# Unread matmuls in seven places of a convolution and mixture-of-experts kernel's head, and a longer SP turn in its planner's account

## The chip, the cores and the metric

The kernel runs on one core of one Trainium2 chip. The metric is device time in microseconds (us) from one execution's start to its end, the median over runs. PE is TensorE (the matrix engine), DVE VectorE, ACT ScalarE, POOL GpSimd and SP SyncE, whose queue issues most of the transfers here.

## The reference

Two steps follow each other. First a causal depthwise convolution of seven taps over 8 sequences of 3584 tokens with 192 channels, whose taps are a softmax of a small weight per head. Then a mixture of experts: each of the 28,672 convolved tokens goes to the one expert of eight with the highest cosine logit, and is weighted by its softmax probability.

```python
x_unf = x_pad[:, idx, :].reshape(B, S, K, H, group)
out = np.einsum('hk,bskhg->bshg', w, x_unf)
...
logits = xn @ en.T / tau
expert_idx = np.argmax(logits, axis=1)
gate_w = probs[np.arange(N), expert_idx]
for e in range(E):
    mask = expert_idx == e
    h = np.maximum(x[mask] @ w1[e], 0.0)
    out[mask] = gate_w[mask, None] * (h @ w2[e])
```

Here `w1` is 192 x 1024 and `w2` 1024 x 192 for each expert.

## The kernel before

The tokens are cut into 16 chunks of 1792. A chunk is convolved on PE against band matrices (`conv`), squared and scaled (`square`, `scales`, `scaled`), split into a high and a low half-precision part (`rest`), transposed, and multiplied by the expert embeddings (`logits`, line 772). `rank` makes ranks and destinations of the logits, and POOL scatters the rows into the DRAM table `rows_d`, sorted by expert. Expert blocks read them back transposed (`rows_of`, line 931) into `xr` or `work`, multiply them by `w1` (line 1100, `h_ps`) and `w2` (line 1122, `o_ps`), and POOL scatters the results to the output (line 1130).

**The head.** The first chunks, the preparation of eight experts' weights and the first eight expert blocks stand in an order written out by hand, the string `HEAD`. Each of its words is one small step: `1c6` is a convolution of chunk 1, `ax1` to `ax3` the trace of a weight's squares and its exponents (expert `a`, lines 369 to 384), `bh1` and `bl1` the high and low parts of a weight, `1t20` a PE transpose, `0g3` a group of logits, `1k3` a stage of the ranks, `z2p0` half of an expert block's first layer, `W6` a weight load. Within each engine the instructions keep the order of the string.

**After the head.** `run` hands out expert blocks step by step and keeps a clock of its own, `self.clock`, that counts PE's planned time. Between the steps it draws pieces of the chunks' routes from `dispatch`. In `route` a chunk's rows are transposed by transfers on SP's queue (`turn`, line 782), and the logits of a group wait, in the plan, until the clock has reached the group's due time:

```python
due[g] = self.queue(SP_TURN, SP_WAIT) + SP_LAND
...
yield due[0]
```

`queue` adds `SP_TURN` to a running time at which SP is free. The plan fixes the order of PE's stream only; on the chip PE waits for the landing itself when the logits come too soon. The account has no other use than these due times, and the due times of chunk 2, whose transposes stand at the end of the head, are zero.

Fourteen matmuls of 128 x 128 by 256 columns that nobody reads stand before the head already (`warm`, line 1262). PSUM is split into rings: `h` with six banks, `l` with one, and `r` with one, which in the kernel before is first used by the convolutions drawn from `dispatch`.

Of the kernel before, what the change touches and what calls it, by code (L numbers as in the profile page):

```python
# [12 lines left out]
F16 = mybir.dt.float16  # L13
F32 = mybir.dt.float32
# [42 lines left out]
SOON = 13  # L57
RANK, GAP = 10.0, 0.5
PE_CONV, PE_LG = 0.64, 0.3
SP_FETCH, SP_TURN, SP_X, SP_WAIT, SP_LAND = 2.8, 2.9, 1.5, 2.5, 3.4  # L60
RAW = 2 * (2 * F + F * D // 128)
AREAS = (1, 2), (1, 1), (1, 0), (0, 1), (1, 1), (1, 0), (0, 1)
HEAD = ("0c0 0c2 0c1 0c5 0c7 0c4 0c6 0c3 0q3 0q7 0q4 0q1 ax1 0q5 0q2 ax2 0q0 0q6 0p "
# [12 lines left out]
AHEAD = 0.4  # L76
HALF = 3 * 2048
SETTLE = 6.0
# [11 lines left out]
def _dep(tc, frm, to, sync=True):  # L90
    cls = mybir.DependencyClass.Sync if sync else mybir.DependencyClass.NoSync
    tc.add_manual_dep(
        frm, to, mybir.DependencyInfo(cls, mybir.DependencyReason.DATA),
        reason="routed rows are written before they are read",
    )
# [15 lines left out]
class _Moe:  # L111
# [473 lines left out]
    def head(self, v):  # L585
        k, a = v[0], v[1:]
        if k in "012":
            c, k, a = int(k), v[1], v[2:]
            if k == "c":
                self.conv(c, int(a), "h")  # L590
            elif k == "q":
                for t in (2 * int(a), 2 * int(a) + 1):
                    self.square(c, t, c or int(a) % 2 == 0)
            elif k == "p":
                self.scales(c)
            elif k == "s":
                self.scaled(c, int(a))
            elif k == "r":
                self.rest(c, int(a))
            elif k == "t":  # L600
                self.flip(c, int(a[0]), int(a[1]))
            elif k == "g":
                if c not in self.lgs:
                    self.lgs[c] = self.ps("l", [128, NT, 2 * E], F32, "lg_ps")
                self.logits(self.lgs[c], self.tiles[c, int(a)], int(a))
            elif k == "v":
                self.roots[c] = self.root(self.mixed[c][3][:])
            elif k == "f":
                self.mixed[c] += self.factor(c),
            else:  # L610
                if k == "k" and a == "1":
                    self.ranks[c] = self.rank(c, self.lgs[c], self.mixed[c][4])
                next(self.ranks[c], None)
        elif k in "abcdefgh":
            e, n = "abcdefgh".index(k), int(a[1])
            if a[0] != "x":
                (self.high if a[0] == "h" else self.low)(e, n - 1)
            elif n < 3:
                self.trace(e, n - 1)
            else:  # L620
                self.exponents(e)
        elif k == "X":
            self.load_x(int(a))
        elif k == "T":
            self.turned = [self.turn(2, g) for g in range(NT // GX)]
        elif k == "W":
            n = int(a)
            self.prep_load(min(n, 7), n - 7 if n > 6 else None)
        elif k == "F":
            self.first_rows("AB".index(a))  # L630
        else:
            e = int(a[0])
            if e not in self.zs:
                self.zs[e] = self.first_block(e)
            next(self.zs[e])


    def rank(self, c, lg, f):
        nc, sp = self.nc, self.sp
# [77 lines left out]
    def by_tile(self, r32):  # L717
# [4 lines left out]
        for i, w in enumerate((self.oneh, self.lth)):  # L722
            nc.tensor.matmul(out=fl(pc[:, 1 - i]), lhsT=w[:TP, :], rhs=fl(self.ohh),
                             start=True, stop=True)
        nc.vector.tensor_copy(out=tot[:, :, 0], in_=self.cb)
        nc.scalar.copy(out=tot[:, :, 1:], in_=pc[:, 1])
        nc.vector.tensor_tensor_scan(out=fl(run), data0=fl(rst), data1=fl(tot),
                                     initial=0.0, op0=ALU.mult, op1=ALU.add)
        have, n = run[:, :, SOON], float(PHASES[1])
# [512 lines left out]
    def run(self):  # L1242
# [15 lines left out]
            self.prep_load(e)  # L1258
        self.embeddings(em, tb)
        warm = self.ps("h", [128, 256], F32, "warm")  # L1260
        for _ in range(WARM):
            i = self.nc.tensor.matmul(out=warm, lhsT=self.idh, rhs=self.onef.bitcast(F16),
                                      start=True, stop=True)
            _dep(self.tc, i.ins, self.em_last, False)
        at = len(self.nc.cur_bb.bb.instructions)
# [11 lines left out]
        a = self.dispatch()  # L1277
# [4 lines left out]
        live, due, done, out = next(a, None), [0.0, 0.0], False, 0.0  # L1282
        while live or self.pend or not done or self.at < len(self.subs):
            if self.at < len(self.subs):
# [5 lines left out]
                for v in self.expert():  # L1290
                    self.steer(spent)
                    self.clock += self.dt
                    out = min(1.0, out + self.pace)
# [54 lines left out]
```

## Time and profile before

| | |
|---|---|
| runs before | 1244.38, 1250.32, 1250.33 us; median 1250.32 us |
| the profiled execution | 1250.26 us, its span 1248.5 us, mean granted clock 0.965 |
| PE busy | 1131.0 us, 91% of the span, in 11202 matmuls |
| DVE, ACT, POOL busy | 642.7, 605.5, 525.3 us |
| transfers | 146.58 MB; share of time of the 16 DMA engines by queue: 38.9% and 14.6% |

The granted clock is the share of TensorE's full clock (2.4 GHz) that the chip allowed: 1.00 is 2.4 GHz and 0.50 is 1.2 GHz, the only two levels here; a value between is a mean over both. Matmuls overlap, so one's duration is longer than the distance to the next; a group's time over its count gives the pace. In rows of the timeline the bracket at the end says how long the engine had been idle before and what it waited for.

### The profile page before, as it was taken

The page shows a single profiled execution, that of the slowest core. Times are in us where ns is not written, and L with a number is a line of the kernel's source. Part 1 is how long each engine was busy: PE and PEld are TensorE (multiplying, and loading weights), DVE is VectorE, ACT ScalarE, POOL GpSimd, SP SyncE. Part 2 cuts the span into 40 slices and gives each one's busy share as a digit, 9 for nine tenths or more (in the row PEclk, how much of TensorE's full clock was granted, in tenths as well). Part 3 has the DMA queues.
Part 4 walks back from the last instruction along what each step waited for, and adds up shares of the span by engine and source line. Part 5 has one row for each costly group of instructions (what it writes and reads, how often), then busy time and mean ns, then how long its engine had stood idle before and what let it go on. Part 6 is the DMA issues. An engine that isn't in the chain of part 4 may idle for free.

```text
span 1248.5 us, 28836 instructions
## 1 busy us (share of the span) xinstructions
PE 1131.0 (91%) x11202; PEld 899.9 (72%) x11202; DVE 642.7 (51%) x1734; ACT 605.5 (49%) x1480; POOL 525.3 (42%) x553
## 2 busy tenths in 40 slices
PE   5775998888989999999999998958999999999997
PEld 3575876667868777667777776736777778788886
DVE  5985656455546456474664646512433344455452
ACT  5984466446445564545554654313444443334332
POOL 3446145445554454555535553563121212222222
PEclk8887999999999999999999999968999999999999
DMA  9968447885996945967678476332022213231210
GB/s 252 277 115 207 102 87 169 168 175 104 183 187 115 192 101 131 202 123 163 133 156 189 90 141 121 85 90 66 24 52 58 52 40 65 58 66 35 51 48 24
DMA packets 324306, 146.58 MB, mean 117 GB/s; under 512 B 266126, under 2 KB 314637, under 8 KB 324160
## 3 DMA queue, kind: packets, MB, share of 16 engines
q1 hardware_dynamic: 300496, 93.97, 38.9%
q0 software_dynamic: 23664, 50.68, 14.6%
q8 instruction: 89, 1.46, 0.5%
q14 instruction: 57, 0.47, 0.1%
HBM read 38.35 MB, written 51.05 MB: 72 GB/s over the span
## 4 chain that ended last, share of the span: by engine, by line
PE 63%; issue 12%; DVE 7%; ACT 5%; DMA 4%; another core or an unknown queue 3%; POOL 3%; SPq 0%; POOLq 0%; ACTq 0%; DVEq 0%
PE h_ps L1100 29%; PE o_ps L1122 26%; PE conv_ps L445 5%; POOL out_dram L1130 3%; DMA xtb<-rows 3%; ACT work L1104 2%; DVE work L1107 2%; DVE res L406 2%; DVE xt L522 1%; PE lg_ps L772 1%; ACT sq L457 1%; DMA xr<-rows_d 1%; ACT rows L527 1%; ACT res L402 0%
## 5 line engine op out<-in xcount | busy, mean ns | idle before, releaser
L1107 DVE SCALAR_TENSOR_TENSOR work<-h_ps,work 128x384 f16<-128x384 f32 (+1 forms) x536 | 320.3, 608 | 494.6 <-ACT work L1104 388.5
L1122 PEld LDWEIGHTS <-work 128*128 128x128 f16 x5472 | 459.8, 98 | 102.2 <-issue 50.2
L1122 PE MATMUL o_ps<-res,work 128*128 128x192 f16 x4992 | 465.5, 248 | 53.3 <-issue 31.1
L1100 PEld LDWEIGHTS <-res 128*128 128x128 f16 x3520 | 310.1, 99 | 163.4 <-issue 25.7
L1104 ACT ACTIVATE work<-h_ps 128x384 f16<-128x384 f32 (+1 forms) x536 | 277.6, 533 | 275.9 <-PE h_ps L1100 200.9
L1130 POOL DMA_INDIRECT out_dram<-y,ids x200 | 203.6, 1018 | 396.2 <-ACT y L1127 366.9
L793 POOL DMA_INDIRECT rows_d<-rows,di x256 | 256.9, 1004 | 183.2 <-ACT work L1104 74.4
L1100 PE MATMUL h_ps<-xr,res 128*128 128x384 f16 (+3 forms) x2280 | 329.6, 300 | 3.2 <-issue 1.6
L1127 ACT ACTIVATE y<-o_ps,gs 128x192 f32<-128x192 f32 x200 | 83.0, 419 | 240.6 <-PE o_ps L1122 175.1
L1100 PE MATMUL h_ps<-work,res 128*128 128x384 f16 (+2 forms) x1240 | 167.7, 288 | 5.8 <-issue 5.7
L445 PE MATMUL conv_ps<-xt,band 128*112 128x384 f32 x256 | 108.3, 514 | 1.3 <-ACT xt L448 0.6
L448 ACT COPY xt<-conv_ps 112x384 f32<-112x384 f32 x128 | 60.7, 480 | 74.8 <-PE conv_ps L445 40.8
L457 ACT ACTIVATE sq<-xt 112x192 bf16<-112x192 f32 x196 | 70.8, 361 | 3.7
L1130 POOL DMA_INDIRECT out_dram<-y,e_mt x20 | 28.1, 1406 | 82.3 <-ACT y L1127 79.5
L522 DVE TENSOR_TENSOR xt<-xt,x_p_s 112x768 f32<-112x768 f32 x64 | 58.7, 946 | 0.0
L527 ACT CAST rows<-xt 112x768 f16<-112x768 f32 x64 | 52.7, 828 | 11.8 <-DVE xt L522 7.2
L534 DVE TENSOR_TENSOR rows<-xt,rows 112x512 f16<-112x512 f32 x64 | 43.9, 686 | 14.2 <-ACT rows L527 9.9
L445 PEld LDWEIGHTS conv_ps<-xt,band 128*112 128x112 f32 x256 | 39.2, 184 | 10.0 <-issue 3.7
L772 PEld LDWEIGHTS <-xtb 128*128 128x128 f16 x768 | 27.7, 96 | 23.6 <-DMA xtb<-rows 13.5
L772 PE MATMUL lg_ps<-ma,xtb 128*128 128x16 f16 x512 | 28.2, 170 | 12.0 <-DMA xtb<-rows 9.4
L457 ACT ACTIVATION_READ_ACCUMULATOR sq<-xt 112x1 f32 x196 | 37.3, 190 | 0.0
L460 DVE SCALAR_TENSOR_TENSOR sq<-xt 112x192 bf16<-112x192 f32 x60 | 21.4, 357 | 19.1 <-ACT xt L448 17.7
(201 smaller groups left out, 651.3 us busy)
## 6 DMA issues: line engine op xcount, KB each, us to landing
xt<-in_dram SPq DMA_DIRECT2D x8, 1536.0 KB
xt<-in_dram SPq DMA_DIRECT2D x7, 1440.0 KB
res<-in_dram SPq DMA_DIRECT2D x6, 768.0 KB
rows_d<-rows,di POOLq DMA_INDIRECT x256
out_dram<-y,ids POOLq DMA_INDIRECT x200
res<-in_dram SPq DMA_DIRECT2D x5, 512.0 KB
xr<-rows_d SPq DMA_TRANSPOSE x154
work<-in_dram SPq DMA_DIRECT2D x3, 512.0 KB
```

The lines of the kernel that those rows point to most:

```text
L445: self.behind(nc.tensor.matmul(out=ps, lhsT=self.band[h], rhs=xt[:, :, h * G:(h + 1) * G], start=True, stop=True))
L457: nc.scalar.activation(out=sq, in_=xc[:, t, :], func=AF.Square, accum_out=n2[:, t:t + 1])
L522: self.nc.vector.tensor_tensor(out=xc[:, u, :], in0=xc[:, u, :], in1=sb, op=ALU.mult)
L527: self.nc.scalar.copy(out=rows[:, u, 128:128 + D], in_=xc[:, u, :])
L772: i = self.nc.tensor.matmul(out=lg[:, g * GX + a, :], lhsT=xT[:, u:u + 128], rhs=self.mb if k == 2 else self.ma, start=(k == 0), stop=(k = ...
L793: i = self.nc.gpsimd.indirect_dma_start(out=self.rows_d[:, :], out_offset=bass.IndirectOffsetOnAxis(ap=idx, axis=0), in_=src, in_offset=No ...
L1100: mm = nc.tensor.matmul(out=ps[:, c, :], lhsT=wa[:, o:o + 128], rhs=xT[:, k, :], start=(i == 0), stop=(i == 4))
L1104: self.step = nc.scalar.activation(out=hh[:, b:b + m, :], in_=ps, func=AF.Relu).ins
L1107: self.last = nc.vector.scalar_tensor_tensor(out=hl[:, b:b + m, :], in0=ps, scalar=0.0, in1=hh[:, b:b + m, :], op0=ALU.max, op1=ALU.subtra ...
L1122: mm = nc.tensor.matmul(out=o, lhsT=h[:, c, q], rhs=w2[:, c, k:k + D], start=(i == 0), stop=(i == len(parts) - 1))
L1127: self.step = nc.scalar.activation(out=y, in_=o, func=AF.Copy, scale=g[a]).ins
L1130: i = nc.gpsimd.indirect_dma_start(out=self.out[:, :], out_offset=bass.IndirectOffsetOnAxis(ap=ids[a], axis=0), in_=y, in_offset=None, bou ...
```

## The change

Words `i22`, `i26`, `i22`, `i12`, `i10`, `i22` and `i12` are put into `HEAD` at seven places, the rest of the string staying in its order. Such a word issues that many matmuls (126 in all) of constants, 128 x 128 by 256 columns, into the one bank of ring `r`; no instruction reads the result. Two constants of the planner's account change: `SP_TURN` from 2.9 to 3.1 and `SP_LAND` from 3.4 to 5.4. Nothing else is edited. The diff shows of `HEAD` only the neighbourhoods of the new words.

```diff
-SP_FETCH, SP_TURN, SP_X, SP_WAIT, SP_LAND = 2.8, 2.9, 1.5, 2.5, 3.4
+SP_FETCH, SP_TURN, SP_X, SP_WAIT, SP_LAND = 2.8, 3.1, 1.5, 2.5, 5.4
...
-  0p ax3 ah1 0s2 0s0 0s3 0t01
+  0p i22 ax3 ah1 0s2 0s0 0s3 i26 0t01
...
-  1q6 1q1 cx3 bl3 dx1 1q4 ch1 ch2 dx2 cl1 1q5 ch3 1q0 dx3
+  1q6 1q1 i22 cx3 bl3 dx1 1q4 ch1 ch2 dx2 cl1 1q5 ch3 1q0 i12 dx3
...
-  W4 ex1 1t11
+  W4 ex1 i10 1t11
...
-  1t02 W6 1t20 fx3 z3m z0p0
+  1t02 W6 i22 1t20 fx3 z3m z0p0
...
-  z2p0 gx1 fh1 1k3
+  z2p0 gx1 fh1 i12 1k3
...
+        elif k == "i":
+            self.busy(int(a))
...
+    def busy(self, n):
+        ps, i = self.ps("r", [128, 256], F32, "warm"), None
+        for _ in range(n):
+            i = self.nc.tensor.matmul(out=ps, lhsT=self.oneh, rhs=self.rhs,
+                                      start=True, stop=True).ins
+        return i
...
+        self.rhs = self.onef.bitcast(F16)
-            i = self.nc.tensor.matmul(out=warm, lhsT=self.idh, rhs=self.onef.bitcast(F16),
+            i = self.nc.tensor.matmul(out=warm, lhsT=self.idh, rhs=self.rhs,
```

## Rows read from the trace of the kernel before

**Rows 1.** Windows: stretch, us, busy PE PEld DVE ACT POOL, clock, DMA, GB/s.

```profile
25.00:50.00 25.00, 18.00 (x203) 13.43 (x204) 21.18 (x59) 23.93 (x52) 9.76 (x14) 0.84 1.05 285
...
825.00:850.00 25.00, 14.86 (x84) 9.13 (x83) 3.34 (x6) 4.09 (x9) 16.59 (x18) 0.70 0.32 86
...
925.00:950.00 25.00, 25.00 (x226) 19.79 (x225) 9.15 (x19) 10.26 (x22) 5.88 (x6) 1.00 0.27 57
```

**Rows 2.** Timeline of PE, head: start, us, what, idle before and releaser.

```profile
22.59 0.35 PE L379 MATMUL n_ps<-w_acc,xr 128*128 128x2 f32 x2 [2.86 <-DVE x_p_e L206]
26.34 0.56 PE L578 MATMUL tr_ps<-xr,rows 112*128 112x112 f16 x4 [3.40 <-ACT rows L527]
...
45.70 0.35 PE L379 MATMUL n_ps<-w_acc,xr 128*128 128x2 f32 x2 [2.93 <-DVE w_dg L372]
...
49.82 0.56 PE L379 MATMUL n_ps<-w_acc,xr 128*128 128x2 f32 x2 [1.63 <-ACT sq L457]
...
58.67 0.37 PE L578 MATMUL tr_ps<-xr,rows 112*128 112x112 f16 x4 [1.64 <-DVE xt L522]
...
71.28 0.53 PE L578 MATMUL tr_ps<-xr,rows 112*128 112x112 f16 x4 [3.17 <-DVE w_dg L372]
...
88.63 0.19 PE L691 MATMUL pc_ps<-rc,lth 112*128 112x8 f16 x1 [1.94 <-DVE rc L685]
```

**Rows 3.** Timeline of PE: two groups of matmuls with 256 columns, and the next.

```profile
8.59 3.17 PE L1262 MATMUL warm<-xr 128*128 128x256 f16 x14
...
135.28 1.25 PE L1100 MATMUL h_ps<-xr,res 128*128 128x256 f16 x10
136.37 0.20 PE L772 MATMUL lg_ps<-ma,xtb 128*128 128x16 f16 x2
```

**Rows 4.** Windows, columns as above: head's stretches at 0.50, and one of three later.

```profile
23.50:30.35 6.85, 4.01 (x28) 3.00 (x29) 6.31 (x10) 6.60 (x13) 5.88 (x11) 0.50 1.07 265
47.40:54.20 6.80, 5.17 (x31) 3.55 (x29) 6.59 (x15) 6.61 (x18) 5.58 (x5) 0.50 0.83 260
71.30:74.70 3.40, 3.40 (x32) 3.40 (x32) 3.37 (x8) 1.81 (x5) 3.15 (x4) 0.50 0.24 45
88.40:91.80 3.40, 3.17 (x32) 3.18 (x33) 3.26 (x11) 2.56 (x8) 0.75 (x1) 0.50 0.51 98
...
224.90:228.30 3.40, 3.40 (x18) 2.43 (x17) 0.00 (x0) 0.93 (x3) 1.22 (x2) 0.50 1.00 194
```

**Rows 5.** Timelines of DVE and ACT in the head: who waits for PE.

```profile
30.91 0.29 DVE L372 SCALAR_TENSOR_TENSOR w_dg<-tr_ps,xr 128x128 bf16<-128x128 f32 x1 [1.10 <-PE tr_ps L369]
...
74.35 0.60 ACT L1104 ACTIVATE work<-h_ps 128x512 f16<-128x512 f32 x1 [1.59 <-PE h_ps L1100]
75.73 0.60 ACT L1104 ACTIVATE work<-h_ps 128x512 f16<-128x512 f32 x1 [0.79 <-PE h_ps L1100]
...
91.03 0.60 ACT L1104 ACTIVATE work<-h_ps 128x512 f16<-128x512 f32 x1 [0.80 <-PE h_ps L1100]
```

**Rows 6.** The chain that ended last, in the head: start, us, what.

```profile
53.01 3.45 DVE res L406 x2
...
67.69 3.26 another core or an unknown queue
```

**Rows 7.** All waits of PE: for what, total us, times, longest.

```profile
PE o_ps L1122 <- issue: 31.1, 35, 3.4
...
PE lg_ps L772 <- DMA xtb<-rows: 9.4, 8, 1.7
...
PE h_ps L1100 <- DMA xr<-rows_d: 1.2, 1, 1.2
```

**Rows 8.** Timeline of PE: the logits with the second longest wait after the head.

```profile
219.18 0.18 PE L772 MATMUL lg_ps<-ma,xtb 128*128 128x16 f16 x1 [1.61 <-DMA xtb<-rows]
```

**Rows 9.** SP's transposes of chunks: ns of one, min/median/max, first and last start.

```profile
L782 SPq DMA_TRANSPOSE xtb<-rows x56: 1407/2120/3762, 108.5 to 769.0; - x56
```

**Rows 10.** Transfers by queue: packets, MB, share; the queue that loads instructions.

```profile
q8 instruction: 89, 1.46, 0.5%
```

25 rows, old and new, of the table HEAD are left out of this document.

## The prediction

> **What bounds the kernel now.** I read the windows of 25 us first. From some 875 us to the end PE is busy all of the time at full clock while DVE, ACT and POOL are half idle [rows 1]; there only the number of matmuls counts, and the change touches none of them. In the head, from 25 to 75 us, DVE and ACT are busy 21 to 24 of 25 us and PE only 18, at a mean clock of 0.84 (the first of two windows that are alike [rows 1]): the head is set by DVE and ACT, with PE behind them. Between, from some 215 to 775 us, PE is again nearly always busy in the page's slices, and its pauses are what can be gained. A third stretch, 825 to 850 us, has PE at 14.86 of 25 us without any engine full but POOL's 16.59 [rows 1]; it holds the largest idle time of the second half. Then I read PE's timeline in the head for the pauses, the windows cut at the changes of the clock, the timelines of DVE and ACT for who waits for PE at all, and last the table of PE's waits for the second half of the change. The sum is made against the profiled execution's 1250.26 us (span 1248.5 us), which is within 0.1 us of the median of the runs.
>
> **The fillers: what they cost.** The words stand ahead of seven matmuls that wait today: for 2.86, 3.40, 2.93, 1.63, 1.64, 3.17 and 1.94 us [rows 2], 17.57 us together. PE runs its stream in order, so a filler that outlasts its pause delays the matmul behind it and all that hangs on it. One filler's price is bounded by the only two groups of 256 columns: 3.17 us over 14 is 0.226 us each, and ten others stand 136.37 - 135.28 = 1.09 us ahead of the next group, 0.109 us each [rows 3]. 256 columns are 0.107 us at 2.4 GHz and 0.213 at 1.2, so the one group ran at the upper level and the other at the lower. So 22, 26, 22, 12, 10, 22 and 12 fillers take 2.4, 2.8, 2.4, 1.3, 1.1, 2.4 and 1.3 us at full clock, and each ends 0.3 to 0.8 us before its pause does: cost zero, hidden by the work of DVE and ACT that ends the pause. At half clock they take 5.0, 5.9, 5.0, 2.7, 2.3, 5.0 and 2.7 us, over by 2.1, 2.5, 2.0, 1.1, 0.6, 1.8 and 0.8: 10.9 us, the upper bound. I take zero and the pace of 0.109, since the first pause begins at full clock (the fall comes at 23.5 [rows 4]) and each filler keeps PE at work until shortly before the next real matmul. No other wait is added: the operands are constants made before the head, the bank of ring `r` has no reader until after the head, and nothing but PE writes it.
>
> **The fillers: what they give.** In the head the clock is at 0.50 in four stretches before 100 us, each behind a pause: 23.5 to 30.35, 47.4 to 54.2, 71.3 to 74.7 and 88.4 to 91.8; PE was at work in them for 4.01, 5.17, 3.40 and 3.17 us, 15.75 in all [rows 4]. If all of it ran at 2.4 GHz, PE would need half, 7.9 us less; that is the upper bound of the gain. But PE's time counts only where somebody waits for it. In the first stretch DVE waits 1.10 us for a trace [rows 5] and PE is in the chain: its 4.01 us become 2.0, so -2.0. In the second nobody waits for PE; the chain there is DVE's low parts of weights [rows 6]: 0. In the third ACT waits 1.59 and 0.79 us for the first expert block [rows 5]: PE's 3.40 become 1.7, -1.7. In the fourth ACT waits 0.80 us [rows 5], while the ranks that POOL waits for are DVE's: -0.4. Together -4.1. Part of the first gain runs into the wait of 3.26 us at 67.69 that ends with no engine's work [rows 6] and may be a landing that comes no sooner. I take -2.5, with ends 0 and -7.9. There is a rule that speaks against even this: the Trainium skill, Perfetto Trace Analysis, section Optimization Strategies, says that when the matmul engine idles for others, one should speed up the engines that block it. By it a filler gives nothing, since no pause gets shorter, and the head's term would be 0 in place of -2.5; the waits of ACT and DVE for PE in rows 5 are what the trace holds against that.
>
> A second stretch of half clock, 105 to 122 us, has no filler near it, and I let it stand.
>
> **The longer turn and landing.** A chunk's first group of logits is now due 2.5 + 2.9 + 3.4 = 8.8 us of the planner's clock after its last piece, then 2.5 + 3.1 + 5.4 = 11.0; if the four turns queue up, the last is due 4 x 0.2 + 2.0 = 2.8 us later. PE waited for these landings 8 times, 9.4 us in all, the longest 1.7 [rows 7, 8]; no wait is as long as the new margin. A turn takes 1.4 to 3.8 us of SP, 2.1 in the median [rows 9]; 2.9 or 3.1 is above that either way, so it is the landing's 2.0 that moves the logits. PE fills the time with expert steps that stand behind the logits today. At most all 9.4 us go. Behind three of these waits, at 187, 225 and 266 us, the clock falls to 0.50 for 3.4 us with PE at work throughout (one shown [rows 4]): 1.7 us each, 5.1 together. Bound: -14.5 us. I take two thirds of the waits and a little under a third of the falls, -6.5 and -1.5, and give 1.0 us back for waits that a new order of PE's stream makes elsewhere: -7.0. The other bound: each of the 13 chunks routed after the head comes out up to 2.8 us later, 36 us if nothing absorbs it. I take nothing of it: PE waited only 1.2 us for rows of the table [rows 7], so the routes run ahead of the blocks.
>
> **Sum.** 1250.26 - 2.5 - 7.0 = 1240.8; I say **1241 us**. With the head's bounds of 0 and -7.9, and -3 to -12 for the landings, this case alone runs from 1231 to 1247.
>
> **The rivals.**
>
> *The head gives nothing, the landings give as said.* DVE is full through 25 to 75 us [rows 1] and takes up what PE saves. 1250.26 - 7.0 = 1243.3 us. Against it: rows 5.
>
> *Only the head gives, or nothing does.* The logits wait less but the same time returns as PE's waits without a shown releaser, which were 31.1 us in 35 pauses at the second layer alone [rows 7], more than three times the waits for landings. 1247.8 to 1250.3 us, no change that can be told.
>
> *The stretch at 825 us moves.* PE was idle 10.1 of 25 us there and at a clock of 0.70 [rows 1]; it is not explained by an engine that is full. PE's instructions come in by 89 packets of 1.46 MB, some 16 KB each [rows 10], and the 126 fillers, each a weight load and a matmul, shift that stream by 252 instructions. The Trainium skill, Runtime: NRT & Kernel Launch, section Instruction fetch mechanics, says that an engine refills in blocks of 256 instructions, mostly hidden. The rows can't tell whether such a load or something else stalls PE here. If the stall goes, its 10.1 us of idle time and some 3 us of the half clock are gone: -13 on top of the sum, 1228 us. If it lengthens, it joins the next case.
>
> *Slower: the routes come too late.* The plan hands out blocks in phases, and the rows of a phase are there when its last chunk is scattered. If 2.8 us per chunk are not absorbed, PE runs dry at each of the eight ends of phases after chunk 3: 8 x 2.8 = 22 us, less the head's 2.5: about 1270 us. It decides from the point at which PE's wait for rows at its first layer passes the 9.4 us that the landings can give. Today it is 1.2 [rows 7].
>
> **How the numbers follow.** My forecast has a chance of 0.45, the first rival 0.10, no change 0.23, the stall that goes 0.12, and slower 0.10. A measurement of this kernel tells no change from about 0.5%, 6.25 us: from 1244.1 to 1256.6. Faster: 0.40 of the forecast's share, 0.06 of the first rival's and 0.12 of the stall's, 0.58. Same: 0.05 + 0.04 + 0.22 = 0.31. Slower: 0.10 and a remnant of 0.01, 0.11. The range of 8 in 10 reaches from 1228, where the stall goes, to 1255, a little past no change; the slower case stays outside.
>
> **What would show it.** Right: in the windows the clock is at 1.00 through 23 to 31, 47 to 54, 71 to 75 and 88 to 92 us; the seven matmuls of rows 2 wait less than 0.8 us each with fillers before them; ACT's work on the first expert block comes before 74.35 us, after a wait of less than 1.59; PE's waits for `xtb<-rows` fall from 9.4 to under 4 us, and the falls at 187, 225 and 266 us are gone. Wrong: a filler still running when its pause should end, at a pace of 0.22 us; the same start of the head's last blocks in spite of a higher clock (DVE took it); a larger wait for `xr<-rows_d`; or a time that is made by the stretch at 812 to 852 us, which nothing in the sum touches.

## The result, and the profile after

The changed kernel takes 1253.26 us in the median of 20 runs, the kernel before 1246.46 us in 20 runs of the same comparison: a ratio of 1.0054, with a 95% interval of 1.0035 to 1.0073. It is slower by 6.8 us, about half a percent. I had forecast 9.3 us less than the profiled execution before (1241 from 1250.26 us); the median of the three runs that I knew then, 1250.32 us, is 3.9 us above that of these 20. The profiled execution took 1254.64 us, 4.4 us more than the one before.

The windows of the changed kernel, at the head's four stretches that stood at 0.50 [rows 4], at the stretch without a filler behind them, and at the stall [rows 1]:

```profile
23.00:31.00 8.00, 6.61 (x84) 5.37 (x81) 7.82 (x16) 8.00 (x16) 6.67 (x12) 1.00 1.08 263
47.00:54.00 7.00, 5.70 (x46) 3.78 (x44) 6.79 (x16) 6.75 (x22) 6.09 (x4) 1.00 1.02 312
71.00:75.00 4.00, 3.62 (x62) 3.62 (x63) 2.45 (x10) 1.77 (x3) 2.97 (x13) 1.00 0.30 57
88.00:92.00 4.00, 3.65 (x54) 3.43 (x52) 3.93 (x8) 3.24 (x14) 2.53 (x2) 1.00 0.45 96
107.60:121.30 13.70, 10.06 (x72) 8.61 (x73) 6.83 (x7) 5.96 (x7) 8.04 (x8) 0.50 1.14 186
...
825.00:850.00 25.00, 15.07 (x84) 8.90 (x83) 2.37 (x5) 3.61 (x8) 16.81 (x18) 0.67 0.25 78
```

The four falls are gone, the later one and the stall stayed. PE's timeline answers rows 2; these are the first two pauses, the fifth and the last, with two groups of fillers:

```profile
22.12 0.35 PE L380 MATMUL n_ps<-w_acc,xr 128*128 128x2 f32 x2 [0.46 <-DVE x_p_e L207]
22.33 3.00 PE L644 MATMUL warm<-xr,oneh 128*128 128x256 f16 x26
25.87 0.37 PE L579 MATMUL tr_ps<-xr,rows 112*128 112x112 f16 x4 [0.54 <-ACT rows L528]
...
57.47 0.37 PE L579 MATMUL tr_ps<-xr,rows 112*128 112x112 f16 x4 [1.76 <-DVE xt L523]
...
85.11 1.48 PE L644 MATMUL warm<-xr,oneh 128*128 128x256 f16 x12
86.72 0.18 PE L701 MATMUL pc_ps<-rc,lth 112*128 112x8 f16 x1
```

26 fillers take 3.00 us, 0.115 each, and end 0.54 us before their pause does. Only ahead of the fifth is still a wait of 1.76 us. The first expert block, which ACT began at 74.35 us [rows 5], begins at 72.71, though ACT's waits for it, 1.80 and 0.52 us, are in sum those of before (1.59 and 0.79):

```profile
72.71 0.60 ACT L1114 ACTIVATE work<-h_ps 128x512 f16<-128x512 f32 x1 [1.80 <-PE h_ps L1110]
73.83 0.60 ACT L1114 ACTIVATE work<-h_ps 128x512 f16<-128x512 f32 x1 [0.52 <-PE h_ps L1110]
```

PE's waits, to be set against rows 7 (for what, total us, times, longest):

```profile
PE o_ps L1132 <- issue: 28.8, 41, 4.1
...
PE lg_ps L782 <- issue: 6.8, 7, 1.3
PE lg_ps L782 <- DMA xtb<-rows: 4.9, 4, 2.1
```

and one more line of the kernel before:

```profile
PE lg_ps L772 <- issue: 1.9, 4, 1.0
```

The waits for landings fell from 9.4 us in 8 to 4.9 in 4. But the logits' waits with no releaser that the profile shows ("issue") rose from 1.9 to 6.8 us, so that both kinds together are 11.3 us before and 11.7 after. The falls of the clock behind the chunks, which I had seen at 187, 225 and 266 us, are there at 189.5, 230.5 and 268, and from 310 to 320 us PE has holes. The turns stayed as they were [rows 9]. One line of SP's transposes, and the windows:

```profile
L792 SPq DMA_TRANSPOSE xtb<-rows x56: 1411/2144/4260, 102.9 to 780.5; - x56
```

```profile
189.50:192.90 3.40, 3.40 (x18) 2.46 (x18) 2.51 (x12) 1.11 (x3) 0.00 (x0) 0.50 1.17 322
230.50:233.90 3.40, 3.40 (x24) 3.23 (x22) 1.38 (x2) 3.24 (x15) 1.88 (x2) 0.51 1.05 160
268.00:274.80 6.80, 5.23 (x26) 3.39 (x25) 0.84 (x3) 1.19 (x3) 1.90 (x2) 0.50 1.06 236
310.00:315.00 5.00, 4.41 (x54) 3.62 (x53) 1.12 (x2) 0.56 (x2) 3.78 (x5) 1.00 0.99 188
315.00:320.00 5.00, 3.38 (x37) 2.69 (x37) 0.69 (x1) 1.77 (x4) 1.54 (x2) 1.00 1.04 222
```

Before, the last two windows were full:

```profile
310.00:315.00 5.00, 4.93 (x77) 4.81 (x75) 1.90 (x5) 1.50 (x4) 3.31 (x4) 1.00 0.97 225
315.00:320.00 5.00, 5.00 (x96) 5.00 (x94) 2.62 (x7) 4.84 (x21) 2.40 (x3) 1.00 0.99 154
```

Where the time went is read best by setting the start of each n-th first-layer weight load of one trace against the same of the other (they come in the same number). After minus before: -1.9 us at 84 us, -5.7 from 145 to 171, -4.3 at 240, -5.7 at 310, +2.7 at 321, +4.9 at 345 and +4.8 at 392, and +4.4 at the end. So the changed kernel was 5.7 us ahead behind the head, and lost 10.6 between 171 and 345 us. Of the 5.7, 2.5 us are one wait of PE for issue in front of `n_ps`, 4.1 us before and 1.6 after, past 95 us: no filler stands there, and before_hold3 below, which has none, is 2.6 us ahead of the kernel before at 171 us as well. Such a curve compares two single executions; and where the order of PE's stream differs, as it does from 201 us on, the order alone shifts it.

The same kernel runs at different speeds on different chips. Six chips (or five: the first is not named) are called A to F in the order in which they came. On A, of this comparison, and on E the kernel before takes 1246.46 and 1244.9 us; on B, C, D and F 1164.26, 1166.01, 1166.01 and 1166.98. So each ratio below is that of one chip, to the kernel before on it.

### The profile page after: what moved, and what is told of

The parts are those of the page before. It is cut to its first block, busy times and chain, and to the rows that moved or that the text cites. A ratio compares the mean times of both kernels' runs of the same rounds, so it can differ in the third digit from the quotient of the medians.

```text
span 1252.9 us, 29088 instructions
## 1 busy us (share of the span) xinstructions
PE 1140.4 (91%) x11328; PEld 907.7 (72%) x11328; DVE 642.4 (51%) x1734; ACT 605.7 (48%) x1480; POOL 528.3 (42%) x553
## 4 chain that ended last, share of the span: by engine, by line
PE 63%; issue 13%; ACT 7%; POOL 5%; DVE 4%; another core or an unknown queue 4%; DMA 3%; SPq 0%; POOLq 0%; ACTq 0%; DVEq 0%
PE h_ps L1110 29%; PE o_ps L1132 27%; PE conv_ps L446 6%; POOL out_dram L1140 3%; ACT work L1114 2%; ACT sq L458 2%; POOL rows_d L803 2%; DMA xtb<-rows 1%; PE lg_ps L782 1%; DVE xt L523 1%; DVE work L1117 1%; ACT rows L528 1%; ACT xtb L582 1%; ACT xt L449 0%
## 5 line engine op out<-in xcount | busy, mean ns | idle before, releaser
L1110 PE MATMUL h_ps<-work,res 128*128 128x384 f16 (+2 forms) x1240 | 164.3, 286 | 4.8 <-issue 3.9
L782 PEld LDWEIGHTS <-xtb 128*128 128x128 f16 x768 | 30.4, 97 | 24.5 <-issue 11.9
```

Source lines behind the costliest of these rows:

```text
L782: i = self.nc.tensor.matmul(out=lg[:, g * GX + a, :], lhsT=xT[:, u:u + 128], rhs=self.mb if k == 2 else self.ma, start=(k == 0), stop=(k = ...
L1110: mm = nc.tensor.matmul(out=ps[:, c, :], lhsT=wa[:, o:o + 128], rhs=xT[:, k, :], start=(i == 0), stop=(i == 4))
```

## The experiments

**Which half costs: chip B.** The fillers alone, the account alone, and the fillers with one of its two numbers.

```diff
 fill_only   SP_TURN, SP_LAND as before (2.9, 3.4), with fillers
 acct_only   SP_TURN, SP_LAND = 3.1, 5.4, without fillers
 fill_turn   SP_TURN, SP_LAND = 3.1, 3.4, with fillers
 fill_land   SP_TURN, SP_LAND = 2.9, 5.4, with fillers
```

> The seven fillers alone, the account of SP's queue as before. Theory (the two parts add up; the head's gain of 5.7 us, seen at 150 us in the changed kernel's trace, stays to the end): 4 to 7 us faster than before, ratio 0.995 to 0.997, and every expert block after the head begins 4 to 7 us earlier. Rival (the gain is lost in any case between 230 and 340 us, at the first chunks routed after the head): within 2 us of before, the blocks from 340 us on within 2 us of their old places.

> The longer turn and landing alone, no fillers. Theory (additive; the later due times cost 10 to 12 us between 230 and 340 us): 9 to 13 us slower than before, ratio 1.007 to 1.010, the head unchanged. Rival (the due times cost only where the fillers have moved the chip against the plan): within 2 us of before. The prediction's own step would give 7 us faster.

> Fillers and the turn of 3.1, the landing back at 3.4. Theory (the landing's 2.0 moves the logits, the turn's 0.2 hardly does): as the fillers alone, 4 to 7 us faster than before. Rival (any new order of PE's stream costs some 10 us, since the old one was chosen by trial): 3 to 7 us slower than before.

> Fillers and the landing of 5.4, the turn back at 2.9. Theory: as the whole change, 4 to 9 us slower than before. Rival (the sum of both is needed): 4 to 7 us faster than before.

Measured: fill_only 1.0004 (0.9992 to 1.0016), acct_only 1.0081 (1.0050 to 1.0111), fill_turn 0.9987 (0.9975 to 1.0000), fill_land 1.0046 (1.0030 to 1.0062). With fillers, it is the landing's 2.0 us that cost, not the turn's 0.2. The fillers alone missed their theory (4 to 7 us faster) and met the rival; fill_turn, 1.4 us faster, met neither of its two; acct_only and fill_land came as expected. The step of the prediction would have had acct_only 7 us faster. It is 9.0 us slower.

**Does the cost grow with the landing: chip C.** Without fillers, the old turn, and 7.4 or 1.4 for the landing; beside them both kernels of the comparison.

```diff
 land_74     SP_TURN, SP_LAND = 2.9, 7.4, without fillers
 land_14     SP_TURN, SP_LAND = 2.9, 1.4, without fillers
```

> The kernel before, unedited, on the chip of this group. Wanted for its trace: on the chip of the first group the fillers alone were at 1.0004 of before, though the traces there put the expert blocks at 160 us 4.3 us earlier with fillers than without. Theory (the head's gain is real and is lost later, because blocks come to a wait that does not move): the blocks at 160 us begin some 4 us later than with the fillers alone, those after the wait at the same time. Rival (before's head is as fast as that with fillers on such a chip): no difference at 160 us. Time: ratio 1.000.

> The changed kernel, unedited, on the same chip. Theory (the parts add up: 1.0004 for the fillers, 1.0081 for the account, each on the first group's chip): ratio 1.004 to 1.009. Rival (the loss belongs to the slower chip of the first pair of traces alone): 0.998 to 1.002.

> No fillers, the turn at 2.9, the landing at 7.4 in place of 3.4: twice the change's step. Theory (what costs is the later place of a chunk's logits, so that the cost grows with the landing): slower than before by more than the account's 0.8%, ratio 1.010 to 1.020. Rival (any other order of PE's stream loses some 5 to 10 us against the one that was chosen, whatever its sign): 1.003 to 1.009.

> No fillers, the turn at 2.9, the landing at 1.4: logits sooner by 2.0 us of plan. Theory (cost grows with the landing, but waits for landings grow below it): between 0.998 and 1.004, with PE's waits for xtb<-rows above the 8 to 9 us of before and the routed chunks' logits earlier in PE's stream. Rival (any other order loses): 1.003 to 1.009 again. The prediction's step, in its mirror (waits for landings are what counts): 1.004 to 1.010, all of it in waits for xtb<-rows.

Measured: before_again 0.9992 (0.9971 to 1.0014), after_again 1.0000 (0.9982 to 1.0018), land_74 0.9983 (0.9964 to 1.0002), land_14 0.9970 (0.9949 to 0.9990). after_again missed its theory and met the rival: on this chip the whole change costs nothing. land_74 and land_14 lie outside every range on record for them. The routes do not come too late in proportion: with 4.0 us more of landing the kernel is no slower. No price per us of landing is seen here, though on a chip where 5.4, with fillers, costs nothing either. Nor do the waits for landings follow the charge: PE waits for them 6.9 us at 1.4 (5.9 on F), 9.3 at 3.4, 5.0 at 5.4 and 4.0 at 7.4. Each value makes an order of its own. Yet in the trace of after_again, as in those of acct_only and fill_land, one step stood out, some 5 to 7 us between 350 and 385 us, and one wait in it: PE for ACT's `work`, 3.9 us in after_again, where before_again has none. That made the next theory.

**The buffer of rows: chip D.** A chunk's rows are laid into one of two buffers, and the buffer is free when the scatters of the chunk two before it have gone out on POOL. The planner starts the rows 5 us of its clock after it has placed the last of these scatters, or later. With a landing of 5.4 chunk 8 starts 0.5 us after that point, as its planner counts. That margin does not set the two kernels apart (in the kernel before it is 0.1 us); the traces below do. after_hold3 lets chunk 8 start 3 us later:

```diff
-        return (c in self.mixed and self.clock >= self.vacant[c % 2]
+        return (c in self.mixed and self.clock >= self.vacant[c % 2] + 3.0 * (c in (8,))
```

> The seven stretches of fillers alone, with the old account, now beside the account alone and the whole change on one chip. Theory of the sum: no filler moves the order of the routed part, and 2 us of the head are given back by 140 us, so ratio 0.998 to 1.001 to the kernel before, here as where it was 1.0004. Rival, the chips differ: on this chip the head's gain reaches the end, ratio 0.994 to 0.997.

> The longer turn and landing alone, no fillers. Theory of the buffer: the new order starts the rows of the seventh routed chunk before the scatters of the chunk two before it have left the buffer; VectorE, and ScalarE behind it, stand 4 to 5 us at about 355 us, TensorE then waits about 4 us for work from ScalarE, and the clock falls after it: ratio 1.003 to 1.009, with this wait in the trace. Rival, the cost that one chip showed (1.0081) was of that chip alone: 0.998 to 1.002, and no such wait.

> The whole change. If the two parts add, its ratio is that of the fillers alone times that of the account alone on this chip, within 0.002. If the fillers also take away what the account costs (they shift when the buffers come free), it is 1.000 while the account alone is 1.005 or more. The wait of VectorE at about 355 us for the scatters of the rows is in the trace by the theory of the buffer, 3 to 5 us.

> The whole change, but the planner lets the rows of the seventh routed chunk (chunk 8) begin 3 us of its clock later; the order of TensorE's stream is the same up to there. Theory of the buffer: the wait of 4 us of VectorE for the scatters at about 355 us, and TensorE's wait behind it, are gone or under 1.5 us, and the time is 3 to 6 us below the whole change on this chip. Rival, the step at 350 us comes from the order in general: the time is within 1.5 us of the whole change, or above it.

Measured: fill_chip3 1.0000 (0.9983 to 1.0017), acct_chip3 1.0041 (1.0021 to 1.0061), after_chip3 1.0027 (1.0004 to 1.0049), after_hold3 0.9974 (0.9957 to 0.9990). The parts add within the intervals, all four met their theories, and the delay takes 4.6 us off the whole change (1166.89 to 1162.26). The timeline of after_chip3, with idle time and releaser:

```profile
352.40 0.94 POOL L803 DMA_INDIRECT rows_d<-rows,di  x1 [0.30 <-issue]
353.64 0.99 POOL L1140 DMA_INDIRECT out_dram<-y,ids  x1 [0.30 <-issue]
354.94 1.00 POOL L1140 DMA_INDIRECT out_dram<-y,ids  x1 [0.31 <-issue]
...
356.29 0.09 DVE L526 MEMSET rows<- 112x32 int32 x1 [5.00 <-DMA out_dram<-y,ids]
...
356.40 0.83 ACT L528 CAST rows<-xt 112x768 f16<-112x768 f32 x1 [4.89 <-DVE rows L526]
...
360.17 2.10 PE L1132 MATMUL o_ps<-res,work 128*128 128x192 f16 x12 [4.75 <-ACT work L1114]
```

POOL issues the last scatter from that buffer at 352.40, ahead of two writes of the output. The memset that opens the buffer for chunk 8 waits for it at the head of DVE's stream, 5.00 us; ACT's cast stands behind that, 4.89 us; ACT's `work` of the expert block stands behind the casts, and PE waits 4.75 us for it. (Here the profile names a write of the output as the memset's releaser; in after_again, acct_chip3 and fill_land, with the same wait, it names the scatter.) In before_again the last of these scatters goes out at 347.68 us and the memset begins at 351.8, without a wait; in after_hold3 at 353.84 and 358.6, without one either. Then, in after_chip3, the clock falls. The windows of after_chip3:

```profile
350.00:355.00 5.00, 5.00 (x60) 4.59 (x58) 1.28 (x3) 0.84 (x2) 3.78 (x5) 1.00 0.67 226
355.00:360.00 5.00, 0.42 (x4) 0.13 (x2) 3.37 (x13) 3.60 (x7) 0.94 (x1) 0.82 0.12 41
360.00:365.00 5.00, 4.83 (x28) 4.21 (x29) 4.86 (x13) 1.76 (x5) 0.00 (x0) 0.50 1.15 156
```

and of after_hold3, on the same chip:

```profile
350.00:355.00 5.00, 5.00 (x66) 4.78 (x64) 3.46 (x14) 1.75 (x4) 3.78 (x4) 1.00 0.95 321
355.00:360.00 5.00, 5.00 (x57) 4.77 (x55) 5.00 (x14) 3.14 (x6) 1.99 (x2) 1.00 0.28 91
360.00:365.00 5.00, 5.00 (x50) 4.33 (x49) 5.00 (x13) 4.12 (x9) 0.49 (x1) 1.00 0.14 25
```

The hole and the fall are gone with the wait. In starts of weight loads after_chip3 loses 7.2 us to before_again between 350 and 385 us, after_hold3 0.4; the same loads on A, where PE has no such wait, show no step (+5.5, +4.8 and +5.8 us). The wait is in all five traces of B, C and D with a landing of 5.4 and no delay, 4.0 to 5.2 us of DVE. land_74 has it smaller: 3.43 us of DVE, 2.11 of ACT and 1.77 of PE. acct_chip3, with the same wait, loses 6.6 us there, and from 285 to 296 us 4.5 more than after_chip3, at one late landing with a fall of the clock behind it:

```profile
288.72 0.21 PE L772 MATMUL lg_ps<-ma,xtb 128*128 128x16 f16 x2 [2.67 <-DMA xtb<-rows]
```

So on D the charge of 5.4 doesn't even keep all landings from being late.

**Is it the wait, or any other order; and where the head's gain goes: chip E.** The same delay in the account alone and in the kernel before, after_hold3 again, and hold3_w8, which is after_hold3 with the word of the last weight load moved up in `HEAD`:

```diff
-  z3m z0p0 FB z4m
+  z3m z0p0 W8 FB z4m
...
-  2s3 2s2 W8 2s0
+  2s3 2s2 2s0
```

With the load that early, hold3_w8 no longer computes all of the reference's output, so this run only shows where the waits go.

> The longer turn and landing alone, without fillers, and the rows of chunk 8 begin 3 us of plan later. Theory of the buffer: the wait of VectorE for the scatters at about 355 us (4.0 us in the account alone) is under 1.5 us, TensorE's wait for ScalarE's work behind it is gone, and 4 to 7 us of the 5 to 9 that the account alone costs are back: ratio 0.998 to 1.002. Rival, any other order: ratio anywhere from 0.997 to 1.010, with the wait or without it.

> The kernel before with the same delay of chunk 8's rows, where the trace shows no wait of VectorE for the scatters between 335 and 372 us. Theory of the buffer: there is nothing to win, ratio 0.998 to 1.003. Rival, a later start of this chunk is better in itself: 0.994 to 0.997, as in the changed kernel.

> The whole change with the delay of chunk 8's rows again, on another chip or another day: ratio 0.995 to 0.999 by the theory of the buffer; 1.000 or more if its gain was of one chip alone.

> As hold3_again, and the last weight load of the head (768 KB) goes into SP's queue ahead of eight transposes that hold it up for 11 to 12 us. Theory that the head's gain is given back to this load: TensorE's wait for it (2 to 4 us at 95 to 99 us) is gone, the first-layer work at 102 us begins 1.5 to 4 us earlier, and at least 1 us of it is left at the end: ratio 0.993 to 0.998, 1 to 3 us below hold3_again. Rival, the transposes behind the load are then late, and what waits for their rows gives it back: no earlier at 138 us, time within 1 us of hold3_again or above.

Measured: acct_hold3 1.0082 (1.0047 to 1.0116), before_hold3 1.0028 (0.9996 to 1.0060), hold3_again 1.0051 (1.0024 to 1.0078), hold3_w8 1.0176 (1.0124 to 1.0229). acct_hold3 and hold3_again missed the theory of the buffer, which would have had both near or below the kernel before; before_hold3 met it. The whole change without the delay was not run on E, so what the delay does there is not measured, but there was little to gain: the changed kernel's trace on A has no wait for the buffer over 2.0 us. So these runs do not test the theory of the buffer; they show that it is not what costs on this kind of chip. All the traces of A and E with a landing of 5.4 have the hole of the changed kernel at 310 to 320 us (acct_hold3 and hold3_again: PE busy 3.16 and 2.84 of the first 5 us; hold3_w8, which is later throughout, at 325 us). The two with 3.4 have not (before_hold3: 5.00).

acct_hold3 and hold3_again differ by the fillers alone, and the kernel with them is 5.9 us faster in the median. The pairs on B (fill_land and acct_only, which also differ by the turn's 0.2) and D (after_chip3 and acct_chip3) lie the same way, by 3.7 and 4.3 us. In each pair the intervals overlap; but beside the longer landing the fillers seem worth more than alone.

As to the head: in hold3_again PE still waits 1.2 us for the load, in hold3_w8 not at all. But the transposes behind it take 13.88 us, where hold3_again's take 11.18, and two other waits open, one of them ACT's for the moved load itself:

```profile
ACT res L402 <- DMA res<-in_dram: 9.3, 1, 9.3
PE pc_ps L700 <- DVE rc L694: 9.3, 1, 9.3
```

The time, 15.5 us above hold3_again, is on the rival's side. But ACT now stands 9.3 us for the load, so what the head would be worth without PE's wait is not shown.

**Twice more: chip F.**

> The fillers alone once more. On a chip where the kernel before takes about 1245 us: if the head's gain of about 6 us is kept while the order of the routed part stays, ratio 0.994 to 0.997; if it is given back there too, 0.999 to 1.002. On a chip where it takes about 1165 us: 0.999 to 1.002, as on the two before.

> Landing charged with 1.4 instead of 3.4, no fillers, old turn. If the account's direction matters and shorter is better: 0.995 to 0.999 on this chip as well. If every account makes its own order and the 0.3% were that order's on that chip: 0.999 to 1.005 here.

Measured: fill_only_2 0.9984 (0.9973 to 0.9995), land_14_2 0.9979 (0.9966 to 0.9991). The fillers alone are 2.2 us faster here, just outside the range that was expected of such a chip. The shorter landing is 0.2 to 0.3% faster on two chips; neither was run where the kernel takes 1245 us, so no version is known to beat both kernels on all chips.

## Why the prediction was wrong

**The step that failed** is the term of the longer turn and landing, -7.0: the account alone costs 9.0 us on B and 5.2 on D (0.8% and 0.4%). Two parts of it were wrong.

The first is the -6.5 of waits that go. On A the waits for landings did fall, by 4.5 us, but the logits' waits without a shown releaser rose by 4.9: 11.3 us of both before, 11.7 after. On E it is the same, 8.9 in before_hold3 against 10.1 in acct_hold3 and 13.0 in hold3_again. So the mechanism of the rival "only the head gives, or nothing does" came true at the logits, though all of PE's waits for issue together rose by 1.4 us only (45.1 to 46.5). (Two thirds of 9.4 are 6.3, not 6.5; nothing hangs on that.) On C, where PE has no such waits, the waits for landings fell by 4.3 us (before_again 9.3, after_again 5.0), and the time stayed (1.0000).

The second is the sentence "give 1.0 us back for waits that a new order of PE's stream makes elsewhere". I looked for a price of the order in rows of the table and in ends of phases (the rival "the routes come too late", 1270 us). It lies in neither: PE's waits for `xr<-rows_d` are 1.2 us before and 1.5 after. On D the price is in good part one collision: two buffers, POOL's queue, DVE's order. I had named nothing that is queued behind a chunk's first DVE instruction, though the memset, the casts and `work` stand in one line there. On C after_again has that collision too and is at 1.0000, so what the wait costs in time is shown by after_hold3 on D alone. That another order alone made its gain is not excluded by a control on such a chip.

**What stays open** is the cause of the loss on A, the chip of the comparison, and on E. The hole at 310 to 320 us is only a part of it. A's curve steps there by 8.4 us, but the same loads step by 5.6 us on C, from before_again to after_again, though PE has no hole there:

```profile
285.00:290.00 5.00, 5.00 (x59) 4.28 (x57) 1.38 (x2) 1.77 (x4) 3.78 (x5) 1.00 1.07 196
290.00:295.00 5.00, 5.00 (x75) 4.24 (x74) 1.04 (x2) 2.59 (x6) 3.42 (x5) 1.00 1.14 246
```

PE's stream is the same on both chips, so those 5.6 us are other work that the new order puts ahead of the loads, and the hole costs some 2.8. From 171 to 310 us the order alone moves C's curve from +0.8 to -6.5; A's stays at -5.7. There some 7 us are lost that I can't put to one wait: PE's pauses there sum to 24.2 us, before to 20.0. Single traces do not carry this further: the kernel before on A and before_hold3 on E have the same PE stream up to 389 us, and before_hold3 goes from 2.6 us ahead at 171 us to 4.0 behind at 240. What stalls PE there was not found.

**The falls behind the chunks.** I had taken 1.5 us for falls that would go; all three stayed. I had put them to the waits for landings; but before, waits for issue stood nearer to two of them (1.17 and 1.35 us ahead of 225, 0.53 and 1.00 ahead of 266), and after, waits for issue of 0.4 to 1.2 us stand ahead of all three, with two waits for landings (1.19 and 1.25 us) ahead of the first and one of 1.73 us for ACT ahead of the last.

**The head** was right in mechanism: the pace (0.115 us), seven pauses of which six shrank as said, four falls gone (fill_chip3 on D has one of 3.4 us instead, at 63.6 us), the first expert block 1.6 us earlier, -1.9 us at 84 us. One sign failed: ACT waits 1.80 us for that block, not less than 1.59, as ACT itself comes to it sooner. The size of -2.5 fits the head, on A and on the other chips (fill_chip3 against before_again: -1.8 at 84). What I missed is the next thing that is late. The chain of the changed kernel through the head has POOL's scatters with gaps of 0.30 us to 62.9 us, then transfers:

```profile
61.91 0.94 POOL rows_d L803
...
63.16 2.78 DMA rows_d<-rows,di
...
66.62 4.72 DMA xr<-rows_d
...
71.38 2.42 PE h_ps L1110 x40
```

and the last weight load stands on SP's queue behind eight transposes until 91.2 us in before_again and 92.5 in after_hold3. Its first matmuls begin between 96.7 and 99.4 us in all 19 traces that keep the place of this load, with fillers or without. A head that is 1.8 us early waits there, and in fill_chip3 again at the first routed block:

```profile
97.44 1.27 PE L370 MATMUL tr_ps<-res 128*128 128x128 bf16 x12 [1.97 <-DMA res<-in_dram]
...
120.96 0.85 PE L1132 MATMUL o_ps<-res,work 128*128 128x192 f16 x8 [3.21 <-ACT work L1114]
```

Held against before_again alone, fill_chip3 has given its lead back by 138 us (1.0 us behind). But before_again has the earliest head of the six traces without fillers on B, C, D and F: at 138 us they lie 0 to 5.0 us behind it, 2.6 in the mean, the eight with fillers from 0.8 ahead to 2.4 behind, 0.7 in the mean. So the lead is 1.9 us in the mean at 138 us as well, and that the load takes it back is not shown. How much of it reaches the end is not settled: the fillers alone are at 1.0004, 1.0000 and 0.9984, from 0.5 us lost to 2.2 us won, and 3.7 to 5.9 us faster beside the longer landing. For the fillers alone the rival "the head gives nothing" came true on B and D and nearly on F. The Trainium skill, Perfetto Trace Analysis, section Optimization Strategies, says to optimize the engines that block the critical path when the matmul engine idles for them. What I took from it, that a filler gives nothing, agrees with these three runs and not with the three pairs. On A the 5.7 us are more than the fillers gave.

**The other rivals.** The stall at 825 us did not move (15.07 of 25 us busy, before 14.86), though one instruction packet more is fetched, 90 for 89. The result lies within the range's upper end, 1255, but on the other side of no change.

## What to carry to other kernels

When a planner's due time is changed, the price is not the due time: count what each moved piece meets on its own engine, the oldest reader of its buffer above all, and what else stands in that engine's order behind it. When a wait is to go, add up all that the same instruction waits for, before and after: here one kind of wait fell and another rose by as much. Set the n-th same instruction of two traces against each other: the difference shows in which stretch a few us were won and lost, which sums of waits don't. But hold it against the same curve of another chip and against several executions, since a new order shifts it where nothing is lost, and two executions of one stream drift apart by several us. And where the order of a kernel is frozen, a half percent of one chip need not be that of another.

## What was not expected of the hardware

The same kernel takes 1245 us on some chips and 1165 on others. In each of the 14 traces of B, C, D and F PE's waits for issue sum to 0.4 us at most; on A they are 45.1 us in 57 waits before and 46.5 in 64 after, on E 45.8 to 55.0. In hold3_again on E, in the stretch of the stall:

```profile
812.05 0.24 PE L1132 MATMUL o_ps<-res,work 128*128 128x192 f16 x1 [1.17 <-issue]
813.45 0.24 PE L1132 MATMUL o_ps<-res,work 128*128 128x192 f16 x1 [1.16 <-issue]
814.88 0.29 PE L1132 MATMUL o_ps<-res,work 128*128 128x192 f16 x1 [1.18 <-issue]
815.59 0.32 PE L1132 MATMUL o_ps<-res,work 128*128 128x192 f16 x1 [0.42 <-issue]
816.30 0.34 PE L1132 MATMUL o_ps<-res,work 128*128 128x192 f16 x1 [0.39 <-issue]
```

One matmul starts each 0.71 or 1.42 us, with nothing that the profile shows to wait for. The windows of the kernel before on C, at the same place:

```profile
803.00:813.00 10.00, 10.00 (x99) 8.39 (x97) 3.56 (x6) 3.72 (x8) 2.51 (x3) 1.00 0.05 19
813.00:830.00 17.00, 17.00 (x142) 12.61 (x141) 8.46 (x15) 7.80 (x17) 3.38 (x4) 1.00 0.08 26
```

It is not the number of instruction loads: 89 packets before on A and on C alike, of 1.1 us each in the median on both. The cause was not found.
